# Low parts of the merged weights behind the product of silu and v, from the second batch on

## The chip, the core and the metric

The kernel runs on one core of one Trainium2 chip. The metric is the device time of one execution in microseconds (us); the median of three runs stands for the kernel. Inside the core five engines work side by side, each through its own instructions in their order: TensorE (PE, matrix products into PSUM; PEld is its weight load), VectorE (DVE), ScalarE (ACT), GpSimd (POOL, which has no access to PSUM) and SyncE (SP, which issues most of the DMAs). An instruction that needs the result of another engine, or a buffer that another engine still reads, waits on a semaphore, and everything behind it on its own engine waits with it.

## The reference

Three layers in a row, all in float32:

```
a = softmax(phi over 32 memory slots);  k_m = a^T k;  v_m = a^T v          # per batch (8) and head (8)
x = softmax(q k_m^T / sqrt(64)) v_m                                        # 576 tokens x 512 per batch
xn = x / sqrt(mean(x*x) + 1e-6) * rms_g
y = (silu(xn @ w_gate) * (xn @ w_val)) @ w_out                             # hidden width 1536
out = relu(y @ w_in2)**2 @ w_out2                                          # hidden width 2048
```

The kernel merges v_m, rms_g and the weights: since x is (attention weights) times v_m, each batch gets its own merged gate and value weights, v_m times w_gate and v_m times w_val, and the attention weights go into them directly.

## The kernel before

A product of two float32 matrices is made of three matrix products with rounded parts: high times high, high times low and low times high. The high part is a rounded copy (ScalarE), the low part the difference to it (VectorE or GpSimd). So every merged weight `wp` that stands in PSUM is copied to `wph` by ScalarE (`wp_hi`, line 544) and then subtracted into `wpl` by VectorE (`wp_lo`, line 550). A chunk `ch` (six of them per batch) has two halves r of 128 x 512, so each of the two steps has two instructions.

The first two layers are one long stage, `phase_a`. Its unit is the *item*: one half batch (288 tokens) and one block of 128 of the 1536 hidden columns. There are 24 items per batch and 192 in all. In one item TensorE makes the gate product `g` (6 matmuls), the value product `v` (6 matmuls, line 804 to 806), and 12 matmuls into `y` for the item two places earlier. ScalarE makes silu(g) into `sl` (line 850), VectorE multiplies it by `v` (line 854, "the product" below), ScalarE and GpSimd split the result into `uh` and `ul` (lines 67 and 71). `g` and `v` have one PSUM bank each: the `v` matmuls of an item wait until the product of the item before has read the bank.

Beside that, the attention part of the *next* batch is made in small steps that are spread over the items by a plan that is written out by hand. An item n has four slots: "a" behind the `g` matmuls, "b" behind the `v` matmuls, "c" behind the product and its split, and "d" behind the `y` matmuls. The plan is a list of (item, slot, step); steps of one slot run in the order of the list. `slot(n, pos)` issues them, and the order in which they are issued is the order on each engine. The steps that matter here, by item number within a batch:

- `wp_mm(ch)` in slot a of the items 14, 16, 18, 20, 22 and 24 (24 is item 0 of the next batch): TensorE makes the merged weights of one chunk in two PSUM tiles (line 532). `wp_ev` in slot b of the same item is `wp_hi` and then `wp_lo`.
- `a13` in slot d of item 13: sum, reciprocal and scaling of the softmax; `a15` in slot c of item 14 and slot a of item 15: VectorE transposes the two halves r of the attention weights into `an` (line 433).
- `a18` in slots b and d of the items 15 and 17: TensorE makes `x` out of `an`, in two PSUM tiles, each with a matmul for r = 0 and one for r = 1 (line 444). `a19`: ScalarE squares them (line 460).
- `p7` in slot c of item 16: VectorE sums the exponentials of the batch after the next (a reduction at line 282 and an addition at line 285).
- `a20` in slot b of the items 19 and 21: TensorE sums the squares into one PSUM tile `ss` (line 473). `a21`: VectorE's reciprocal root, in two parts; the second part (lines 500 to 503) stands in slot c of the items 20 and 22. `a23` in slot a of item 21 and slot c of item 23 scales `an` (line 510).

All these small TensorE results (`wp`, `x`, `ss`, and others of the attention) share one pair of PSUM banks, the tag "att" with two buffers (line 214), in strict rotation. So a matmul that writes such a tile waits until the tile before the last of the same tag has been read to the end. Between the items 14 and 24 the order of the tiles is: wp(14) two, x(15 b) two, x(15 d) two, wp(16) two, x(17 b) two, x(17 d) two, wp(18) two, ss(19) one, wp(20) two, ss(21) one, wp(22) two, wp(24) two. A `wp` tile is read to the end when `wp_lo` has read it.

The weights of the first batch are handled apart: their `wp_hi` stands in slot c and their `wp_lo` in slot d already (line 703). Conversions of the raw weights (`conv_next`, lines 101 to 115) fill other slots of VectorE, ScalarE and GpSimd.

Of the kernel before, what the change touches and what calls it, by code (L numbers as in the profile page):

```python
# [52 lines left out]
class Kernel:  # L53
# [496 lines left out]
            self.nc.vector.tensor_tensor(lo[:, r], t, self.wph[b, ch][:, r].bitcast(F32), op=ALU.subtract)  # L550
        self.wpl[b, ch] = lo

    def wp_ev(self, b, ch):
        self.wp_hi(b, ch)
        self.wp_lo(b, ch)


    def conv_start(self):
        if self.conv_keys:
# [42 lines left out]
    def make_plan(self):  # L602
        self.early, self.warm_ps = 0, None
        self.w1, self.wo, self.wph, self.wpl, self.anh, self.anl = {}, {}, {}, {}, {}, {}


        groups = [(0, hf, fs) for fs in (range(NF1 // 2), range(NF1 // 2, NF1)) for hf in range(2)]
        groups += [(b, hf, range(NF1)) for b in range(1, B) for hf in range(2)]
        self.items = [(b, hf, f, f == fs[0], f == fs[-1]) for b, hf, fs in groups for f in fs]

        def gv(ch):
            return [(kind, ch, cp) for kind in "gv" for cp in range(2)]

        def o(*fs):
            return [("o", f, 0) for f in fs]

        keys = gv(0) + gv(1) + o(0, 1) + gv(2) + o(2, 3, 4, 5) + gv(3) + gv(4) + o(6, 7) + gv(5) + o(8, 9, 10, 11)
        keys += [(c, f, 0) for f in range(NF2) for c in "iz"]
        self.raw_keys, self.conv_keys = keys, list(keys)

        self.plan = {}

        def at(n, pos, step, b, *args):
            if b < B:
                self.plan.setdefault((n, pos), []).append((step, (b, *args)))


        steps = [
            (1, "a", 0, "a7", 0),
            (1, "a", 0, "load_q", 2),  # L630
            (1, "d", 0, "t1"),
            (1, "d", 0, "a3", 0),
            (2, "a", 0, "a7", 1),
            (2, "a", 0, "load_q", 3),
            (2, "b", 0, "a2"),
            (2, "c", 0, "a3", 1),
            (2, "d", 0, "a4"),
            (0, "d", 1, "load_phi"),
            (3, "b", 0, "a5"),
            (3, "c", 0, "a6"),  # L640
            (3, "c", 0, "a7", 2),
            (3, "d", 1, "load_kv", 0),
            (4, "c", 0, "a7", 3),
            (4, "d", 1, "load_kv", 1),
            (5, "b", 0, "a8", 0),
            (5, "c", 0, "a9", 0),
            (5, "d", 1, "load_q", 0),
            (6, "b", 0, "a8", 1),
            (6, "c", 0, "a9", 1),
            (6, "d", 1, "load_q", 1),  # L650
            (7, "c", 1, "p1"),
            (8, "c", 0, "a10", 0),
            (9, "b", 1, "p3"),
            (9, "c", 0, "a10", 1),
            (11, "b", 1, "p4"),
            (11, "c", 1, "p5"),
            (12, "a", 0, "a12", 0),
            (12, "a", 0, "a12", 1),
            (12, "a", 1, "p6"),
            (13, "b", 0, "a13", 0),  # L660
            (13, "d", 0, "a13", 1),
            (14, "c", 0, "a15", 0),
            (15, "a", 0, "a15", 1),
            (15, "b", 0, "a18", 0, 0),
            (15, "c", 0, "a19", 0, 0),
            (15, "d", 0, "a18", 0, 1),
            (15, "d", 0, "a19", 0, 1),
            (16, "c", 0, "sq_add", 0),
            (16, "c", 1, "p7"),
            (17, "b", 0, "a18", 1, 0),  # L670
            (17, "c", 0, "a19", 1, 0),
            (17, "d", 0, "a18", 1, 1),
            (17, "d", 0, "a19", 1, 1),
            (18, "c", 0, "sq_add", 1),
            (19, "b", 0, "a20", 0),
            (19, "c", 0, "a21", 0, 0),
            (20, "c", 0, "a21", 0, 1),
            (21, "a", 0, "a23", 0),
            (21, "b", 0, "a20", 1),
            (21, "b", 0, "an_split", 0),  # L680
            (21, "c", 0, "a21", 1, 0),
            (22, "c", 0, "a21", 1, 1),
            (23, "c", 0, "a23", 1),
            (24, "d", 0, "an_split", 1),
        ]
        for ch in range(NCH):
            i = 14 + 2 * ch
            steps += [(i - 3, "d", 0, "wst_load", ch), (i, "a", 0, "wp_mm", ch), (i, "b", 0, "wp_ev", ch)]

        at(1, "c", "a21", 0, 1)  # L690
        at(2, "a", "a23", 0, 1)
        at(2, "d", "an_split", 0, 1)
        for b in range(B - 1):
            for i, pos, ahead, step, *args in steps:
                if (b, step) == (0, "t1"):
                    step = "t1_first"
                at(NI * b + i, pos, step, b + 1 + ahead, *args)
        at(0, "c", "p6", 1)

        for n, ch in ((1, 1), (3, 2), (7, 3), (10, 4), (13, 5)):  # L700
            at(n, "c", "wp_mm", 0, ch)
            at(n, "c", "wp_hi", 0, ch)
            at(n, "d", "wp_lo", 0, ch)
# [550 lines left out]
```

## Time and profile before

| | us |
|---|---|
| median of 3 runs (lowest to highest) | 1626.82 (1623.26 to 1627.28) |
| the profiled execution: its own time, its span | 1628.49, 1626.7 |
| TensorE busy, share of the span | 1556.0, 96% |
| VectorE busy | 1015.5, 62% |
| ScalarE busy | 592.6, 36% |
| GpSimd busy | 392.8, 24% |

All rows of the profile are from the one profiled execution; the span runs from its first to its last instruction, and the execution's own time is 1.8 us longer. A row of the timeline has the start in us, the duration in us, engine, line, operation, output and inputs, shapes, the number of instructions that it merges, and in brackets how long the engine had stood idle before and what ended that. TensorE runs its matmuls in a pipeline, so their durations overlap; one 128x288 matmul starts 0.13 us behind the one before. `phase_a` with the attention of later batches fills the stretch from about 60 to 800 us; the items 14 to 24 of a batch come seven times in it, about 97 us apart.

### The profile page before, as it was taken

Reading aid. Unit: us, or ns where it says so; the run is one execution under the profiler, and the core shown is the slowest. Engines: PE = TensorE matmul, PEld = TensorE weight load, DVE = VectorE, ACT = ScalarE, POOL = GpSimd, SP = SyncE. Lnnn points to the kernel's source line nnn. Section 1 sums busy time; section 2 is a strip of 40 time slices with the busy share of each in tenths; the row PEclk is TensorE's granted clock in tenths of the full one; section 3 lists DMA queues with packets and bytes.
Section 4 is the critical chain, followed back from the end, with each engine's and each line's share of the span. In section 5 each row is a group of like instructions: output and inputs, shape, how many; then the busy total and the mean of one; then the engine's idle time right before and its main releaser. Section 6 shows DMA issues by size and latency. Waiting matters only on the chain.

```text
span 1626.7 us, 26611 instructions
## 1 busy us (share of the span) xinstructions
PE 1556.0 (96%) x10298; PEld 1308.7 (80%) x10298; DVE 1015.5 (62%) x1713; ACT 592.6 (36%) x1208; POOL 392.8 (24%) x415
## 2 busy tenths in 40 slices
PE   6587999999999999999999999999999999999998
PEld 3365798897978889798998887888788878887887
DVE  4987764757456574733546876666566665666465
ACT  2566535444353544434343323211331133112322
POOL 0476634434343443524322210000000000000000
PEclk7698899999999999999999999999999999999999
DMA  9897674454837545423223566344534453545352
GB/s 248 268 275 281 224 211 172 156 169 181 230 132 221 180 157 154 162 71 119 80 74 121 185 219 191 109 152 153 177 122 143 162 181 99 167 161 176 94 167 97
DMA packets 143023, 269.94 MB, mean 166 GB/s; under 512 B 30704, under 2 KB 72944, under 8 KB 136752
## 3 DMA queue, kind: packets, MB, share of 16 engines
q1 hardware_dynamic: 129440, 248.43, 46.9%
q10 hardware_dynamic: 13328, 19.54, 3.9%
q8 instruction: 81, 1.33, 0.3%
q14 instruction: 46, 0.38, 0.1%
q0 software_dynamic: 128, 0.26, 0.1%
HBM read 208.28 MB, written 59.90 MB: 165 GB/s over the span
## 4 chain that ended last, share of the span: by engine, by line
PE 83%; DVE 6%; ACT 3%; DMA 3%; POOL 2%; issue 2%; SPq 0%; ACTq 0%; POOLq 0%; DVEq 0%
PE y L820 5%; PE y L821 5%; PE y L822 5%; PE z L1177 5%; PE z L1179 4%; PE z L1178 4%; PE h_S L1013 4%; PE h_S L1011 4%; PE h_S L1012 4%; PE zz L1179 3%; PE h_A L1011 3%; PE v L804 3%; PE zz L1178 3%; PE zz L1177 3%; PE h_A L1013 3%; PE h_A L1012 3%
## 5 line engine op out<-in xcount | busy, mean ns | idle before, releaser
L71 POOL TENSOR_TENSOR ul<-sl,uh 128x288 fp32r<-128x288 f32 x192 | 166.6, 868 | 367.5 <-ACT uh L67 366.4
L820 PE MATMUL y<-uh,woh 128*128 128x288 f32 x768 | 236.0, 307 | 0.0
L821 PE MATMUL y<-uh,wol 128*128 128x288 f32 x768 | 228.1, 297 | 0.8 <-POOL wol L71 0.8
L822 PE MATMUL y<-ul,woh 128*128 128x288 f32 x768 | 227.1, 296 | 0.0
L67 ACT ACTIVATE gh<-c 128x512 fp32r<-128x512 f32 (+1 forms) x96 | 53.8, 561 | 404.0 <-DVE c L1046 399.7
L854 DVE TENSOR_TENSOR sl<-sl,v 128x288 f32<-128x288 f32 x192 | 86.1, 448 | 177.5 <-PE v L806 137.9
L1185 POOL DMA_DIRECT2D out_dram<-os_last x4 | 2.2, 554 | 656.4 <-DVE os_last L1196 656.4
L820 PEld LDWEIGHTS y<-uh,woh 128*128 128x128 f32 x768 | 145.3, 189 | 17.2 <-issue 16.3
L67 ACT ACTIVATE uh<-sl 128x288 fp32r<-128x288 f32 x192 | 85.2, 444 | 182.5 <-DVE sl L854 182.5
L821 PEld LDWEIGHTS y<-uh,wol 128*128 128x128 f32 x768 | 145.8, 190 | 1.7 <-POOL wol L71 1.0
L822 PEld LDWEIGHTS y<-ul,woh 128*128 128x128 f32 x768 | 145.4, 189 | 0.0
L850 ACT ACTIVATE sl<-g 128x288 f32<-128x288 f32 x192 | 78.7, 410 | 165.3 <-PE g L806 162.7
L804 PE MATMUL g<-anh,wph 128*128 128x288 f32 x384 | 119.1, 310 | 12.9 <-ACT sl L850 10.9
L1177 PE MATMUL z<-bzh,gh 128*128 128x512 f32 x320 | 126.1, 394 | 0.0
L804 PE MATMUL v<-anh,wph 128*128 128x288 f32 x384 | 119.6, 311 | 6.6 <-DVE sl L854 6.6
L1179 PE MATMUL z<-bzh,gl 128*128 128x512 f32 x320 | 125.8, 393 | 0.0
L1178 PE MATMUL z<-bzl,gh 128*128 128x512 f32 x320 | 125.0, 391 | 0.0
L805 PE MATMUL g<-anl,wph 128*128 128x288 f32 x384 | 114.7, 299 | 0.1
L805 PE MATMUL v<-anl,wph 128*128 128x288 f32 x384 | 114.5, 298 | 0.0
L806 PE MATMUL v<-anh,wpl 128*128 128x288 f32 x384 | 114.0, 297 | 0.0
L806 PE MATMUL g<-anh,wpl 128*128 128x288 f32 x384 | 113.5, 296 | 0.0
L550 DVE TENSOR_TENSOR wpl<-wp,wph 128x512 fp32r<-128x512 f32 x96 | 61.3, 680 | 77.4 <-ACT wph L544 77.4
(222 smaller groups left out, 3816.7 us busy)
## 6 DMA issues: line engine op xcount, KB each, us to landing
w<-w SPq DMA_DIRECT2D x48, 1024.0 KB, 6.3
si<-w_i SPq DMA_DIRECT2D x80, 256.0 KB, 2.8
q<-in_q_dram SPq DMA_DIRECT2D x128, 144.0 KB, 5.0
gd<-c SPq DMA_DIRECT2D x64, 256.0 KB, 2.0
gb<-gd ACTq DMA_DIRECT2D x64, 256.0 KB, 3.8
y<-ys SPq DMA_DIRECT2D x16, 576.0 KB, 3.2
raw_i<-in_moe_w_in_dram SPq DMA_DIRECT2D x16, 512.0 KB, 4.0
raw_z<-in_moe_w_out_dram SPq DMA_DIRECT2D x16, 512.0 KB, 3.8
```

What stands on the lines that cost most here:

```text
L67: nc.scalar.activation(hi, src, AF.Copy)
L71: eng.tensor_tensor(lo, src, hi.bitcast(F32), op=ALU.subtract)
L804: nc.tensor.matmul(out, wh[:, r, cs], ah[:, r], start=(r == 0), stop=False)
L805: nc.tensor.matmul(out, wh[:, r, cs], al[:, r], start=False, stop=False)
L806: nc.tensor.matmul(out, wl[:, r, cs], ah[:, r], start=False, stop=(r == NR - 1))
L820: nc.tensor.matmul(y, hi[:, cs], uh, start=first, stop=False)
L821: nc.tensor.matmul(y, lo[:, cs], uh, start=False, stop=False)
L822: nc.tensor.matmul(y, hi[:, cs], ul, start=False, stop=last)
L1011: nc.tensor.matmul(out, wh[:, cs], xh, start=(kk == 0), stop=False)
L1177: nc.tensor.matmul(y[c], gh[:, cs], oh, start=(f == 0), stop=False)
L1178: nc.tensor.matmul(y[c], gh[:, cs], ol, start=False, stop=False)
L1179: nc.tensor.matmul(y[c], gl[:, cs], oh, start=False, stop=(f == NF2 - 1))
```

## The change

`wp_ev` goes. `wp_hi` stays in slot b. `wp_lo` goes to slot c of the same item: on VectorE it is issued behind the product of that item, and, since the plan's list has it last, behind all other steps of that slot. No instruction is added or taken away, and the first batch keeps its order.

```diff
-    def wp_ev(self, b, ch):
-        self.wp_hi(b, ch)
-        self.wp_lo(b, ch)
...
         for ch in range(NCH):
             i = 14 + 2 * ch
-            steps += [(i - 3, "d", 0, "wst_load", ch), (i, "a", 0, "wp_mm", ch), (i, "b", 0, "wp_ev", ch)]
+            steps += [(i - 3, "d", 0, "wst_load", ch), (i, "a", 0, "wp_mm", ch)]
+            steps += [(i, "b", 0, "wp_hi", ch), (i, "c", 0, "wp_lo", ch)]
```

In slot c of these items VectorE then has ahead of `wp_lo`: in item 14 one transpose (`a15`), in item 16 the two instructions of `p7`, in items 20 and 22 the four instructions of `a21`'s second part, in items 18 and 24 nothing.

## Rows read from the trace of the kernel before

**Rows 1.** The page: its head and the busy time of each engine.
```profile
span 1626.7 us, 26611 instructions
PE 1556.0 (96%) x10298; PEld 1308.7 (80%) x10298; DVE 1015.5 (62%) x1713; ACT 592.6 (36%) x1208; POOL 392.8 (24%) x415
```

**Rows 2.** TensorE's waits, 150 to 300 us: us in total, times, longest.
```profile
PE v L804 <- DVE sl L854: 1.0, 1, 1.0
```

**Rows 3.** TensorE's waits, 300 to 800 us.
```profile
PE v L804 <- DVE sl L854: 4.1, 4, 1.0
```

**Rows 4.** Timeline of VectorE in the items 14 and 15 of one batch.
```profile
364.43 1.22 DVE L550 TENSOR_TENSOR wpl<-wp,wph 128x512 fp32r<-128x512 f32 x2
365.57 0.44 DVE L854 TENSOR_TENSOR sl<-sl,v 128x288 f32<-128x288 f32 x1
365.93 1.43 DVE L433 STREAM_TRANSPOSE an<-L 128x576 f32<-128x576 f32 x2
```

**Rows 5.** Timeline of TensorE in item 15 of that batch.
```profile
364.75 0.29 PE L806 MATMUL g<-anh,wpl 128*128 128x288 f32 x1
366.07 0.40 PE L804 MATMUL v<-anh,wph 128*128 128x288 f32 x1 [1.02 <-DVE sl L854]
367.05 1.07 PE L444 MATMUL x<-an,kvz 32*64 32x288 f32 x8
368.05 0.40 PE L820 MATMUL y<-uh,woh 128*128 128x288 f32 x1
```

**Rows 6.** Timeline of VectorE in the items 16 and 17 of that batch.
```profile
373.32 1.29 DVE L550 TENSOR_TENSOR wpl<-wp,wph 128x512 fp32r<-128x512 f32 x2 [4.56 <-ACT wph L544]
374.53 0.44 DVE L854 TENSOR_TENSOR sl<-sl,v 128x288 f32<-128x288 f32 x1
...
376.96 0.42 DVE L285 TENSOR_TENSOR es<-es,ph 64x256 f32<-64x256 f32 x1
377.31 0.44 DVE L854 TENSOR_TENSOR sl<-sl,v 128x288 f32<-128x288 f32 x1
```

**Rows 7.** Timeline of TensorE in the items 16 and 17 of that batch.
```profile
373.30 0.29 PE L806 MATMUL v<-anh,wpl 128*128 128x288 f32 x1
...
376.73 0.71 PE L444 MATMUL x<-an,kvz 32*64 32x288 f32 x8
377.38 0.40 PE L820 MATMUL y<-uh,woh 128*128 128x288 f32 x1
```

**Rows 8.** Timeline of an undisturbed item: last matmul of v, and the product.
```profile
240.13 0.29 PE L806 MATMUL v<-anh,wpl 128*128 128x288 f32 x1
...
240.53 0.45 DVE L854 TENSOR_TENSOR sl<-sl,v 128x288 f32<-128x288 f32 x1 [1.20 <-PE v L806]
```

**Rows 9.** Timeline of TensorE in the first batch of the seven, item 17.
```profile
181.40 0.85 PE L444 MATMUL x<-an,kvz 32*64 32x288 f32 x6 [1.57 <-ACT sq L460]
```

**Rows 10.** Timeline of VectorE in item 20 of the batch of rows 4.
```profile
390.93 1.28 DVE L550 TENSOR_TENSOR wpl<-wp,wph 128x512 fp32r<-128x512 f32 x2
392.13 0.44 DVE L854 TENSOR_TENSOR sl<-sl,v 128x288 f32<-128x288 f32 x1
...
393.46 0.94 DVE L502 SCALAR_TENSOR_TENSOR sqt<-sqt 128x288 f32<-128x288 f32 x1
394.44 0.46 DVE L503 SCALAR_TENSOR_TENSOR sq<-sqt,sq 128x288 f32<-128x288 f32 x1
```

**Rows 11.** Timeline of TensorE in the items 20 and 21 of that batch.
```profile
390.63 0.29 PE L806 MATMUL v<-anh,wpl 128*128 128x288 f32 x1
...
393.95 0.65 PE L473 MATMUL ss<-sq,ones 128*128 128x288 f32 x2
```

**Rows 12.** Timeline of GpSimd in item 20 of that batch.
```profile
393.12 0.97 POOL L71 TENSOR_TENSOR ul<-sl,uh 128x288 fp32r<-128x288 f32 x1 [2.29 <-ACT uh L67]
```

**Rows 13.** Three stretches: length, busy time of each engine, granted TensorE clock, DMA.
```profile
181.94:188.76 6.82, 6.39 (x35) 3.54 (x30) 2.26 (x3) 3.75 (x8) 4.50 (x4) 0.50 0.35 112
270.68:274.10 3.42, 3.42 (x20) 2.69 (x19) 0.42 (x2) 1.04 (x3) 2.03 (x2) 0.50 0.86 317
366.00:369.40 3.40, 3.33 (x24) 2.56 (x25) 2.73 (x6) 2.49 (x6) 1.74 (x2) 1.00 1.03 374
```

## The prediction

> **What bounds the kernel now.** I read the page first: TensorE is busy in 96% of the span, VectorE in 62% [rows 1]. So an edit on VectorE counts only through a wait that it puts on TensorE or takes from it. Therefore I went to the list of TensorE's waits, cut to the stretch in which the moved step runs. It names one wait that comes back: the v matmuls wait for a product, once between 150 and 300 us and four times between 300 and 800, 5.1 us in all [rows 2, 3]. From 300 us on no row of that list names `wp_lo` as the releaser. Last I read the timelines of VectorE and TensorE around this wait, and around each place where TensorE needs a buffer that `wp_lo` frees. All of the sum below is from there.
>
> **The change part by part.** Nothing is added: 84 subtractions (seven batches, six chunks, two halves) change places on VectorE. On the other engines the order stays. `wp_lo` feeds the g and v matmuls only ten items later, so its results aren't urgent. Two other things are: the product, which comes earlier, and the two "att" banks, which come free later.
>
> When may the product run? In an undisturbed item it starts 0.40 us after the start of the last v matmul (240.13 to 240.53) [rows 8]. A released matmul starts 0.06 us after its releaser's end: the product of item 14 ends at 365.57 + 0.44 = 366.01, v starts at 366.07 [rows 4, 5]. A pair of subtractions takes 1.28 us, and since the next instruction starts 0.08 before its forerunner's end, each takes (1.28 + 0.08) / 2 = 0.68 [rows 10].
>
> *Item 14, the wait that goes.* VectorE is late here, and works without a break from 364.43: two subtractions, product, two transposes, done at 367.36 [rows 4]. Afterwards the order is product, first transpose, two subtractions, second transpose. The product then ends at 364.87, so v, whose g matmuls are done at about 365.0, no longer waits, and 1.02 us are gone. What is late next? The x matmuls right behind v. Their second one reads the second half of `an`, and that transpose still ends at 367.36, since the same five instructions stand ahead of its end. The rows show that it binds already: from the start of x to the next y it takes 1.00 us (367.05 to 368.05), in item 17 only 0.65 (376.73 to 377.38) [rows 5, 7]. So y starts at 368.05 as before, and the wait has only moved from v to x. I take 0. The ends: 1.02 us gained in each of the five cases, if x were free; 0.1 lost in each, if a transpose gets slower.
>
> *Item 16, a new wait.* Here VectorE had been idle for 4.56 us and began the subtractions as soon as the high part was there, 373.32. Now it starts with the product, and that needs v: 373.30 + 0.40 = 373.70 [rows 6, 7]. From there product and `p7` take 2.78 us (374.53 to 377.31) [rows 6], so the subtractions begin at 376.48 and end at about 377.77 instead of 374.61. But item 17 writes x into the same two banks. It started at 376.73 [rows 7]. Its first tile now waits until 376.48 + 0.68 + 0.06 = 377.22, its second until 377.83. The second half of x takes half of 0.65 us, so y follows at 378.16 instead of 377.38: 0.78 us lost, on TensorE itself, with nothing beside it. Queued on VectorE behind the subtractions is the product of item 17, 0.38 us later than before (the time that VectorE now waits for v); its v bank is not wanted before item 18. `p7` exists for six of the seven batches. In the first of them x in slot d of item 17 already waits 1.57 us, on squares that stand behind that product [rows 9]; it swallows the 0.78 and I count 0.38 there. Together 5 x 0.78 + 0.38 = 4.3 us. The ends per batch: 0.40, if the 0.38 were not lost; 1.58, if the addition in `p7`, 0.42 us here, had to stand aside for a GpSimd operation of 0.8 us.
>
> *Item 20, a second new wait.* The product may start at 390.63 + 0.40 = 391.03 (VectorE is free at 390.93) [rows 10, 11]. From the start of the product to the end of `a21`'s four operations it took 394.44 + 0.46 - 392.13 = 2.77 us, less 0.08 for the overlap (390.93 + 1.28 to 392.13) [rows 10]. So the subtractions start at 393.72, the first ends at 394.40, and ss in item 21, which takes the bank of the first half, starts at 394.46 instead of 393.95 [rows 11]: 0.51 us lost, seven times, 3.6 us. The ends per batch: 0.03, if the slow operation of 0.94 us took 0.46 like its neighbour; 1.0, if another one became as slow.
>
> The Trainium skill has a rule that speaks against this change. "SBUF — State Buffer", section "SBUF: two separate sides", says that VectorE and GpSimd share a pair of ports as an exclusive lock: a VectorE operation with two SBUF inputs and a GpSimd operation that reads SBUF shut each other out for a whole instruction. The slow operation agrees: 0.94 us at 393.46, while GpSimd works from 393.12 to 394.09 [rows 10, 12]. Its result is the fourth rival.
>
> *Items 18, 22 and 24: 0.* In item 18 nothing stands between product and subtractions, so they end 0.4 us later, and the next user of the bank comes more than an item later. In item 22 the same four operations of `a21` are in between, but the next user is item 24, with a whole item of y, g and v ahead of it (24 matmuls at 0.13 us, 3.1 us). In item 24 the next user is in slot d of the following item.
>
> *Earlier uh and ul: 0.* They follow the product and come up to 1.1 us earlier, but the matmuls that read them stand two items later and wait for neither.
>
> The sum is 4.3 + 3.6 = 7.9 us against the profiled execution's own 1628.49, so 1636.4. That execution lies 1.7 above the median of 1626.82; against the median I predict 1634.7. Both new waits repeat in every batch relative to TensorE's own work, so no later slack takes them back: the chain of items 12 to 14 starts from a product of item 11 and shifts with TensorE.
>
> **The rivals.**
>
> 1. *Faster.* The wait of item 14 goes and x doesn't take its place. For it: 5 x 1.02 = 5.1 us are there to be had [rows 2, 3]. It decides on whether the second transpose is done by the time x's second matmul could run, about 366.2; it would have to end 1.16 us before its 367.36, though VectorE has no idle time to give. Without the two new waits the time is 1626.82 - 5.1 = 1621.7.
>
> 2. *No change.* The matmuls of items 17 and 21 don't meet the later subtractions, because their bank isn't the one in question or was waited for anyway. Against it stands the strict rotation of two; the gap between v and x in item 17 shows no wait that could cover one. 1626.8.
>
> 3. *One of the two.* Only p7 or only a21 delays far enough: the wait of item 20 is 0.51 us, and its lower end is 0.03. 1626.82 + 4.3 = 1631.1, or 1630.4 with the other one.
>
> 4. *Operations that shut each other out.* Moved operations of VectorE meet GpSimd where they didn't: 0.8 us more on `p7` in five batches and 0.5 more on `a21` in seven, 7.5 us: 1642.2. Against it: the GpSimd operations that they met follow the same product, so they come earlier by about as much. It is what the skill's rule on the lock would make of the move at its worst.
>
> 5. *The clock.* After stalls the granted clock stood at half, 1.2 GHz, for 6.82 us in the first batch, and for 3.42 us behind one of the five waits on the product; behind the wait of rows 5 it stayed at 2.4 GHz [rows 5, 13]. 3.42 us at half cost about 1.7 us of full-speed work. The new waits are shorter than that one, but there are 13. Four more such falls: 1634.7 + 6.8 = 1641.5.
>
> **How the numbers follow.** Forecast 0.60, faster 0.08, no change 0.10, one of the two 0.10, shut out 0.07, clock 0.05. The forecast's own range is 1632 to 1639: one clock stretch of 3.42 us gone or one or two added, and the 3.6 us by which the lowest of three runs lies under the median. For 8 in 10 I take 1629 to 1640.5; it takes in the third rival and leaves the first, the second and most of the last two out. What a measurement of this kernel can tell from no change is about 0.3%, 4.9 us. Slower by more than that (over 1631.7): nearly all of the forecast, the last two, and a little of the third, 0.73. Within it: the second, most of the third and the forecast's lower edge, 0.18. Faster: the first, and a chance gain of clock stretches beside the second, 0.09.
>
> **What would show it.** In the changed trace the five waits of v on the product are gone, and x waits for `an` about as long in the same items. x waits for `wpl` in item 17 of five batches, 0.5 us before the first tile, and y starts 0.8 us later behind v than before. ss waits for `wpl` in item 21, about 0.5 us. A batch of the middle is 1.3 us longer. The forecast is wrong if the waits on `wpl` are missing, or if y in item 15 comes earlier behind g.

## The result and the profile after

| | before | after |
|---|---|---|
| median of 6 runs (lowest to highest), us | 1626.6 (1623.26 to 1629.8) | 1634.0 (1632.19 to 1639.69) |
| the profiled execution: its own time, its span, us | 1628.49, 1626.7 | 1635.25, 1633.4 |

The ratio is 1.0054, with a 95% interval of 1.0040 to 1.0068: the changed kernel is slower by 0.5%, 7.4 us between the medians. The forecast was 1634.7.

The page of the changed kernel, head and busy times, against [rows 1]:

```profile
span 1633.4 us, 26640 instructions
PE 1558.6 (95%) x10298; PEld 1308.7 (80%) x10298; DVE 1016.3 (62%) x1713; ACT 592.8 (36%) x1208; POOL 392.9 (24%) x415
```

VectorE, ScalarE and GpSimd are as busy as before, within 1 us. The span is 6.7 us longer, and TensorE's busy time rises by only 2.6: an x that is let go in two steps, shown below, counts as busy for longer. The rest went into waits. The list of TensorE's waits, 300 to 800 us, against [rows 3]:

```profile
PE x L444 <- DVE wpl L550: 3.3, 8, 0.5
PE ss L473 <- DVE wpl L550: 2.3, 5, 0.5
PE x L444 <- DVE an L433: 2.1, 4, 0.5
```

The four waits of v on the product are gone. In their place x waits for the second transpose, four times too, and two releasers are new, both the low parts: for x and for ss. VectorE in the items 14 and 15 of the batch that [rows 4] shows:

```profile
364.56 0.40 DVE L851 TENSOR_TENSOR sl<-sl,v 128x288 f32<-128x288 f32 x1
364.87 0.77 DVE L433 STREAM_TRANSPOSE an<-L 128x576 f32<-128x576 f32 x1
365.56 1.25 DVE L550 TENSOR_TENSOR wpl<-wp,wph 128x512 fp32r<-128x512 f32 x2
366.73 0.76 DVE L433 STREAM_TRANSPOSE an<-L 128x576 f32<-128x576 f32 x1
```

and TensorE there, against [rows 5]:

```profile
364.88 0.29 PE L803 MATMUL g<-anh,wpl 128*128 128x288 f32 x1
365.01 0.40 PE L801 MATMUL v<-anh,wph 128*128 128x288 f32 x1
...
366.35 0.67 PE L444 MATMUL x<-an,kvz 32*64 32x288 f32 x2 [0.28 <-DVE wpl L550]
367.54 0.71 PE L444 MATMUL x<-an,kvz 32*64 32x288 f32 x6 [0.52 <-DVE an L433]
368.18 0.40 PE L817 MATMUL y<-uh,woh 128*128 128x288 f32 x1
```

Now v follows g at once. But the second transpose ends at 366.73 + 0.76 = 367.49, and x goes on at 367.54. From VectorE's first instruction here to the next y it is 368.18 - 364.56 = 3.62 us, as it was 368.05 - 364.43 = 3.62.

VectorE in the items 16 and 17, against [rows 6]:

```profile
373.82 0.46 DVE L851 TENSOR_TENSOR sl<-sl,v 128x288 f32<-128x288 f32 x1 [4.93 <-PE v L803]
374.19 2.07 DVE L282 TENSOR_REDUCE es<-ph 128x256 f32<-128x1024 f32 x1
376.30 0.42 DVE L285 TENSOR_TENSOR es<-es,ph 64x256 f32<-64x256 f32 x1
376.64 1.27 DVE L550 TENSOR_TENSOR wpl<-wp,wph 128x512 fp32r<-128x512 f32 x2
```

and TensorE, against [rows 7]:

```profile
376.63 0.29 PE L803 MATMUL v<-anh,wpl 128*128 128x288 f32 x1
377.46 1.30 PE L444 MATMUL x<-an,kvz 32*64 32x288 f32 x8 [0.54 <-DVE wpl L550]
378.69 0.40 PE L817 MATMUL y<-uh,woh 128*128 128x288 f32 x1
```

The low parts end at 376.64 + 1.27 = 377.91, behind `p7`. x starts 0.83 us behind the start of the last v matmul and takes 1.23 us to the next y instead of 0.65. The second pair of its four matmuls alone, cut out by a window that leaves the first pair out:

```profile
378.06 0.70 PE L444 MATMUL x<-an,kvz 32*64 32x288 f32 x4
```

VectorE in item 20, against [rows 10]:

```profile
392.35 0.46 DVE L851 TENSOR_TENSOR sl<-sl,v 128x288 f32<-128x288 f32 x1 [0.25 <-PE v L803]
...
393.70 0.94 DVE L502 SCALAR_TENSOR_TENSOR sqt<-sqt 128x288 f32<-128x288 f32 x1
394.68 0.46 DVE L503 SCALAR_TENSOR_TENSOR sq<-sqt,sq 128x288 f32<-128x288 f32 x1
395.06 1.28 DVE L550 TENSOR_TENSOR wpl<-wp,wph 128x512 fp32r<-128x512 f32 x2
```

and TensorE in item 21, against [rows 11]:

```profile
395.13 0.29 PE L803 MATMUL v<-anh,wpl 128*128 128x288 f32 x1
395.89 0.72 PE L473 MATMUL ss<-sq,ones 128*128 128x288 f32 x2 [0.47 <-DVE wpl L550]
396.24 0.51 PE L817 MATMUL y<-uh,woh 128*128 128x288 f32 x1
```

The low parts begin only when `a21` is done, and ss finds its bank unread. Before, the last v matmuls stood so ahead of x and of ss, and the next y so behind ss:

```profile
376.51 0.29 PE L806 MATMUL v<-anh,wpl 128*128 128x288 f32 x1
...
393.81 0.29 PE L806 MATMUL v<-anh,wpl 128*128 128x288 f32 x1
...
394.21 0.51 PE L820 MATMUL y<-uh,woh 128*128 128x288 f32 x1
```

that is, x came 0.22 us behind the first and ss 0.14 behind the second [rows 7, 11]; now it is 0.83 and 0.76.

The starts of v are the best clock for such a comparison. The table takes, for each kernel of this study, the median over the second to the sixth of the seven batches (us between the starts of v):

| kernel | item 14 to 16 | item 17 to 18 | item 21 to 22 | median of all runs |
|---|---|---|---|---|
| before | 10.92 | 5.96 | 4.78 | 1626.6 |
| changed | 10.93 | 7.16 | 5.47 | 1634.0 |
| only item 16 | 10.92 | 7.15 | 4.80 | 1631.76 |
| only item 20 | 10.91 | 5.96 | 5.47 | 1630.46 |
| items 14, 18, 22, 24 | 10.94 | 5.96 | 4.77 | 1625.62 |
| low parts first in slot c | 10.91 | 6.51 | 4.77 | 1627.35 |
| halves parted in item 16 | 10.92 | 7.29 | 5.48 | 1634.21 (one run) |
| before, conversion moved | 9.24 | 5.96 | 4.77 | 1615.74 |
| low parts first, conversion moved | 9.33 | 6.50 | 4.77 | 1619.09 |
| changed, conversion moved | 9.34 | 7.16 | 5.48 | 1626.45 |

Per batch of the middle the change costs 1.20 us at item 17, 0.69 at item 21 and nothing at item 14.

### The profile page after: what moved, and what is told of

The parts are those of the page before. It is cut to its first block, busy times and chain, and to the rows that moved or that the text cites. A ratio compares the mean times of both kernels' runs of the same rounds, so it can differ in the third digit from the quotient of the medians.

```text
span 1633.4 us, 26640 instructions
## 1 busy us (share of the span) xinstructions
PE 1558.6 (95%) x10298; PEld 1308.7 (80%) x10298; DVE 1016.3 (62%) x1713; ACT 592.8 (36%) x1208; POOL 392.9 (24%) x415
## 4 chain that ended last, share of the span: by engine, by line
PE 80%; DVE 10%; ACT 3%; DMA 2%; issue 2%; POOL 2%; SPq 0%; ACTq 0%; DVEq 0%; POOLq 0%
PE y L817 5%; PE y L818 5%; PE y L819 5%; PE z L1174 4%; PE z L1176 4%; PE z L1175 4%; PE h_S L1008 4%; PE h_S L1010 4%; PE h_S L1009 4%; PE zz L1176 4%; PE zz L1175 4%; PE zz L1174 4%; PE h_A L1008 3%; PE h_A L1010 3%; PE h_A L1009 3%; PE v L801 3%
## 5 line engine op out<-in xcount | busy, mean ns | idle before, releaser
L1043 DVE SCALAR_TENSOR_TENSOR c<-c 128x512 f32<-128x512 f32 (+1 forms) x160 | 102.9, 643 | 4.1
```

## The experiments

In some of the expectations the stretches of 5.96 (later 7.15) and 4.77 us are said to start at item 16 and item 20; they are the ones of the table, from item 17 and from item 21. The first four kernels ran beside 32 runs of the kernel before (median 1626.25), the others beside 17 (1625.28), and the ratios are taken against these.

**One place at a time.** The first three kernels split the change by chunks (`{...}` is 1, then 3, then 0, 2, 4 and 5):

```diff
-            steps += [(i - 3, "d", 0, "wst_load", ch), (i, "a", 0, "wp_mm", ch), (i, "b", 0, "wp_ev", ch)]
+            steps += [(i - 3, "d", 0, "wst_load", ch), (i, "a", 0, "wp_mm", ch)]
+            steps += [(i, "b", 0, "wp_hi", ch), (i, "c" if ch in {...} else "b", 0, "wp_lo", ch)]
```

Item 16 alone:

> Only the chunk of item 16 has its low parts behind the product; all others stay as before. Theory (the time is lost where x in item 17 finds its two banks still unread): from v of item 16 to v of item 18 a batch takes 7.16 us instead of 5.96 in the five middle batches, all other stretches as before, five waits of v on the product stay; 5 x 1.2 and a little of the first batch, about +6.4 us, 1633. Rival (the loss is spread over all moved chunks, since VectorE is later everywhere): a sixth of the loss, +1.3 us, 1628.

Measured: 1631.76, ratio 1.0039 (1.0023 to 1.0054). TensorE's waits, 300 to 800 us:

```profile
PE v L805 <- DVE sl L855: 4.1, 4, 1.0
PE x L444 <- DVE wpl L550: 2.2, 4, 0.5
```

The old wait is still there, x's new one has come, ss has none.

Item 20 alone:

> Only the chunk of item 20 moves. Theory: ss in item 21 waits for the first half, from v of item 20 to v of item 22 less any wait on a weight load 5.47 us instead of 4.77 in seven batches, +4.9 us, 1631.5. Rival (spread): +1.3 us, 1628.

Measured: 1630.46, ratio 1.0030 (1.0018 to 1.0042). The same list:

```profile
PE v L805 <- DVE sl L855: 4.1, 4, 1.0
PE ss L473 <- DVE wpl L550: 2.3, 5, 0.5
```

The other four:

> The chunks of the items 14, 18, 22 and 24 move, those of 16 and 20 stay. Theory: the five waits of v on the product (1.0 us each) go and come back in front of x in the same item, since the second transpose ends no earlier; v of item 14 to v of item 16 takes 10.9 us as before; 1626.6, no change. Rival (item 14 gains and the other places hid it): 5 x 1.0 us less, 1621.5.

Measured: 1625.62, ratio 0.9998 (0.9988 to 1.0008). The same list:

```profile
PE x L444 <- DVE an L433: 2.1, 4, 0.5
PE x L444 <- DVE wpl L550: 1.2, 4, 0.3
```

So two places carry the loss, and each carries its own: a spread over all six would have given each of the first two 0.09% or so. Item 14 gains nothing: the wait is only handed on. The three ratios add up to 1.0067, against 1.0054 for the whole; the intervals cover the difference.

**Behind the product, but first in its slot.** `wp_lo` is put at the head of the plan's list, so that only the product stands between `wp_hi` and it:

```diff
-            steps += [(i, "b", 0, "wp_hi", ch), (i, "c", 0, "wp_lo", ch)]
+            steps += [(i, "b", 0, "wp_hi", ch)]
+            steps.insert(ch, (i, "c", 0, "wp_lo", ch))
```

> All six chunks move behind the product, but the low parts come first in slot c, ahead of a15, p7 and a21's second part. Theory: the banks come free 0.35 us later than before the change and no matmul waits for that; the waits on the low parts in the items 17 and 21 are gone, the wait of item 14 still only moves from v to x; 1626.6, as the kernel before. Rival (being behind the product is itself what costs): 1634, as the changed kernel.

Measured: 1627.35, ratio 1.0008 (1.0000 to 1.0017). Most of the loss is gone, so it was the queue of slot c and not the place behind the product that cost it. But the theory expected nothing at all in item 17, and 0.55 us per batch are left. VectorE in the items 16 and 17 of this kernel:

```profile
376.74 0.89 DVE L285 TENSOR_TENSOR es<-es,ph 64x256 f32<-64x256 f32 x1
377.55 0.44 DVE L852 TENSOR_TENSOR sl<-sl,v 128x288 f32<-128x288 f32 x1
```

GpSimd beside it:

```profile
376.55 0.80 POOL L468 TENSOR_TENSOR sq<-sq,sqt 128x288 f32<-128x288 f32 x1
```

ScalarE behind the product:

```profile
378.02 0.44 ACT L67 ACTIVATE uh<-sl 128x288 fp32r<-128x288 f32 x1 [2.10 <-DVE sl L852]
378.37 0.69 ACT L460 ACTIVATE sq<-x 128x288 f32<-128x288 f32 x2
```

and TensorE in slot d of item 17:

```profile
378.82 1.00 PE L444 MATMUL x<-an,kvz 32*64 32x288 f32 x8 [0.18 <-ACT sq L460]
```

`p7`'s addition takes 0.89 us instead of 0.42, beside a GpSimd operation that ends at 377.35. The product comes late, `uh` and the squares behind it too, and the second x waits for the squares' banks. It waits only 0.18 us, but it then takes 1.00 instead of 0.71, its banks having come free one after the other. The lock that the Trainium skill states ("SBUF — State Buffer", "SBUF: two separate sides") agrees with these rows: the addition has two SBUF inputs, the GpSimd operation started first, and the addition ends 0.28 us behind it. No run takes that GpSimd operation away, so its part in the longer addition is read from the overlap and not shown.

**Which release counts?** In item 16 the first half of the low parts goes ahead of `p7`, the second stays behind it:

```diff
+            if ch == 1:
+                steps += [(i, "b", 0, "wp_hi", ch), (i, "c", 0, "wp_lo_half", ch, 1)]
+                steps.insert(0, (i, "c", 0, "wp_lo_half", ch, 0))
```

> As the changed kernel, but in item 16 the two halves are parted: product, first half, p7, second half. So the first bank of x in item 17 is free long before x, the second as late as in the changed kernel. Theory (the loss hangs on the last release alone: the four matmuls of x run side by side only if all are let go together, and a pair let go later takes the full 0.63 us by itself): v of item 16 to v of item 18 stays at 7.15 us. Rival (the prediction's reading, half of x costs half of 0.65, and the first pair's wait counts by itself): the stretch falls by 0.3 us, to 6.85.

Measured: 1634.21 in its one run, and 7.29 us for the stretch (a slower addition of `p7`, 0.56 us, lies in it). TensorE in item 17:

```profile
375.07 0.70 PE L444 MATMUL x<-an,kvz 32*64 32x288 f32 x4
376.41 0.70 PE L444 MATMUL x<-an,kvz 32*64 32x288 f32 x4 [0.64 <-DVE wpl L558]
377.04 0.40 PE L829 MATMUL y<-uh,woh 128*128 128x288 f32 x1
```

The first two of the four matmuls run early and help nothing: the other two still take 377.04 - 376.41 = 0.63 us to the next y, hardly less than the 0.65 of all four together in [rows 7].

**The lateness itself.** Why is VectorE late in item 14? In front of it stand the two operations of a weight conversion, in slot c of item 13. Three kernels, the one before, the one with the low parts first and the changed one, have that conversion in item 5, with its steps on ScalarE and GpSimd:

```diff
-        elif NI <= n < NI * (B - 1) and pos == "c" and n % NI == NF1 + 1:
+        elif NI <= n < NI * (B - 1) and pos == "c" and n % NI == 5:
```

> The kernel before, with the weight conversion of slot c of item 13 moved to slot c of item 5 of the same batch. Theory (VectorE is late in item 14 because of the two operations of that conversion, 1.29 and 1.18 us): the wait of v on the product and the wait of x on an go both, v of item 14 to v of item 16 falls from 10.9 us to the 9.24 of the last batch, which has no conversions; 5 x 1.67 = 8.3 us less, 1618. Rival (the stall comes from the sums of the softmax or turns up at item 5): no change, 1626.

Measured: 1615.74, ratio 0.9945 (0.9931 to 0.9959), faster than both kernels. What is left of TensorE's waits between 300 and 800 us:

```profile
PE wp L532 <- DMA w<-w: 0.5, 2, 0.3
```

VectorE in item 14:

```profile
359.04 1.29 DVE L550 TENSOR_TENSOR wpl<-wp,wph 128x512 fp32r<-128x512 f32 x2 [0.80 <-ACT wph L544]
360.24 0.44 DVE L854 TENSOR_TENSOR sl<-sl,v 128x288 f32<-128x288 f32 x1
```

In the old order of low parts and product VectorE now even waits 0.80 us for the high part, and item 14 to 16 takes 9.24 us, as it does in the seventh batch of the kernel before, which has no conversion there.

The conversion makes VectorE late by more than its own work. VectorE in item 13 of the kernel before, ahead of [rows 4]:

```profile
360.30 1.29 DVE L110 TENSOR_SCALAR cv_z<-cv_z 128x512 uint32<-128x512 uint32 x1
361.63 1.18 DVE L111 SCALAR_TENSOR_TENSOR cv_z<-raw_z,cv_z 128x512 uint32<-128x512 uint32 x1
...
363.50 0.71 DVE L423 TENSOR_SCALAR ls<-ls 128x18 f32<-128x18 f32 x1
```

and GpSimd beside it, last with the conversion's own step:

```profile
360.15 1.16 POOL L425 TENSOR_TENSOR L<-L,ls 128x576 f32<-128x576 f32 x1 [0.62 <-DVE ls L424]
361.27 0.99 POOL L71 TENSOR_TENSOR ul<-sl,uh 128x288 fp32r<-128x288 f32 x1
362.88 1.30 POOL L115 TENSOR_TENSOR cv_z<-cv_z,cr_z 128x512 int32<-128x512 int32 x1 [0.62 <-DVE cv_z L111]
```

With the conversion in item 5 its two operations take 0.67 and 0.69 us (at 328.18 and 328.88), and the third one, a step of the softmax sums that stays in item 13, takes 0.27 (at 357.67). So 3.18 us became 1.63: about half of VectorE's time in these three operations was that they took longer there, beside GpSimd. The move takes the operations and this lengthening out of item 13 together, and no run parts the two.

> The low parts first in slot c, and the conversion moved as above. Theory: the same 8.3 us less than with the low parts first alone, 1619, and no better than the kernel before with the conversion moved: once VectorE isn't late, the order of product and low parts is worth nothing. Rival (an earlier product is worth something): 1 us or more faster than that kernel.

Measured: 1619.09, ratio 0.9963 (0.9950 to 0.9976). No better than with the old order, and 3.4 us slower: the 0.54 us of item 17 have stayed, 2.7 us in five batches, and 0.09 has come at item 14.

> The changed kernel, and the conversion moved as above. Theory: the new waits of the items 17 and 21 stay (7.15 and 5.47 us), the stall of item 15 goes: 1634 - 8.3 = 1625.7. Rival (the new waits come from VectorE's lateness since item 13 and go with it): 1618.

Measured: 1626.45, ratio 1.0007 (0.9998 to 1.0015). The waits on the low parts have not moved, 7.16 and 5.48 us, so they do not come from the lateness of item 13. That the time equals the kernel before's is a sum of a gain and a loss of equal size. Against the kernel before with the same move the change costs 1626.45 - 1615.74 = 10.7 us.

## Why the prediction was right

*Item 14, 0.* Right. The wait of 1.02 us went and came back in front of x, at the transpose that the prediction named. The faster rival fails at its own condition.

*Item 16, 0.78 us.* Right in place and sign, too small: 1.20. The start of the low parts (2.78 us behind the product; measured 376.64 - 373.82 = 2.82) and their end were right. The mis-sized term is "the second half of x takes half of 0.65 us". The four matmuls of x run side by side when they are let go together; a pair that is let go by itself still takes 0.63 (378.06 to 378.69; it starts 0.15 us behind the end of the low parts). That is 0.30 of the missing 0.42; 0.09 more is the release, 0.15 us instead of the 0.06 of a product's, the rest the start of the low parts.

*Item 20, 0.51 us.* Right in place, 0.69 measured: again a release of 0.15 (395.06 + 0.68 to 395.89) instead of 0.06, and ss to y takes 0.35 us instead of 0.26 after the wait.

*The sum.* By these sizes the loss is 5 x 1.20 + 7 x 0.69 = 10.8 us; 7.9 were predicted, and the medians differ by 7.4. The two profiles show where the difference to 10.8 went in these two executions: from the v of item 14 of the first of the seven batches to that of item 14 of the eighth batch, which has none of these steps, the changed kernel takes 8.6 us more. 1.5 us of the difference to 10.8 are a stretch of half clock in the second batch [rows 13] that the changed kernel's profile doesn't have. Another 1.65 is one wait for a weight load in the third, which only the kernel before has:

```profile
PE wp L532 <- DMA w<-w: 1.6, 1, 1.6
```

The first batch adds 1.65 instead of 0.69: 10.8 - 1.5 - 1.65 + 0.95 = 8.6. Ahead of that the profile of the changed kernel is 2.0 us earlier, in code that is the same in both; in the ten profiles of the study this v starts between 158.4 and 161.5 us. For the medians nothing shows such an account: the interval of the ratio is 6.5 to 11.1 us, which takes in 10.8, and with the conversion moved the change costs 10.7. So the total of 7.9 came out closer than its two terms, 4.3 for 6.0 and 3.6 for 4.8, and that is luck.

*The rivals.* "One of the two" and "no change" fall with the first two experiments. The operations that shut each other out did not decide the changed kernel: `p7`'s addition took 0.42 us as before, and a conversion step that became slower (1.18 us at 386.43, 0.69 at 384.62 before) holds up no matmul. `p7`'s addition took longer in three other kernels, 0.87 to 0.89 us in the two with the low parts first and 0.56 with the halves parted. The new waits brought no fall of the clock in the changed kernel's profile. A stretch of it as in [rows 13], one of seven of about 98 us each from 187.2 to 873 us:

```profile
285.00:383.00 98.00, 96.18 (x840) 83.84 (x832) 59.15 (x103) 43.67 (x95) 41.31 (x44) 1.00 0.56 180
```

The granted clock is 1.00 in all seven, 2.4 GHz through all batches but the first; by an estimate, (98 - 1.71) / 98, a fall of 3.42 us would give 0.98 in one of them. A fall can also follow the wait of item 15 in its new form: in the profile of the kernel that moves the items 14, 18, 22 and 24 the clock stood at half from about 657.2 to 660.7 us, behind the waits of 0.29 and 0.52 us in item 15 of the sixth batch, and item 14 to 16 took 12.39 us there.

## What to carry to other kernels

A step that is moved behind another one in the text is moved behind everything that the same slot issues on that engine; look which buffer it frees, who takes that buffer next in the rotation, and how long the new queue ahead of it is. A wait that goes gives nothing if the same late engine also feeds the next instruction: ask what made it late, and move that. Do not price a late half of a group of small matmuls at half the group's time: here two of the four x matmuls by themselves took nearly as long as all four.

## What the runs showed of the hardware

The four matmuls of x, each on 32 rows and 64 columns of the array, run side by side when they are let go together. In the kernel before, four of their eight instructions start at 376.73 and are done 0.47 us later:

```profile
376.73 0.47 PE L444 MATMUL x<-an,kvz 32*64 32x288 f32 x4
```

All four matmuls take 0.65 us to the next instruction, two alone 0.63. From 300 to 800 us a matmul that waits for a buffer which the low parts free started 0.15 us behind their end in every case, one that waits for a product or for squares 0.05. What releases is not all: x that waits for a transpose started 0.05 to 0.06 us behind it in the changed kernel, and 0.14 with the low parts first (365.35 + 0.77 to 366.26). No run here tells why.
